# Causal attention with a soft mixture of experts: routing products moved to the idle score place, one maximum transposition for a pair of heads, a fourth buffer for raw q and k

## The chip, the cores and the metric

The kernel runs on one core of one Trainium2 chip. A core has five engines that run side by side and wait for each other by semaphores: TensorE (PE; its weight loads are listed apart as PEld), VectorE (DVE), ScalarE (ACT), GpSimd (POOL) and SyncE (SP), which here issues nearly all DMAs. SBUF holds the operands, and matrix products land in PSUM, which has eight banks of 512 float32 columns on 128 partitions. The metric is the device time of one execution in microseconds (us).

## The reference

```python
# q, k, v: (8, 12, 448, 64); phi: (768, 32); w1: (8, 768, 1024); w2: (8, 1024, 768)
scores = q @ k.T / 8, masked above the diagonal with -1e9       # each of 96 heads
attn = exp(scores - scores.max(-1)); attn /= attn.sum(-1) + 1e-9
x = (attn @ v), heads side by side                               # (3584, 768)
logits = x @ phi                                                 # (3584, 32)
d = softmax of logits over the 3584 rows;  slot_input = d.T @ x  # (32, 768)
slot_out = relu(slot_input @ w1[e]) @ w2[e]                      # 4 slots for each of 8 experts
out = (softmax of logits over the 32 slots) @ slot_out           # (3584, 768)
```

## The kernel before

Heads go in pairs: 48 pairs `p`, six for each of the eight batch rows, and one call of `block(p)` for each. Heads are numbered `i`; block `p` finishes heads `a = 2p` and `a + 1` and prepares heads `a + 2` and `a + 3`. `m6 = p % 6` says which of the six pairs of a batch row it is. Every engine runs its instructions in the order in which the code is written (`_InOrder`).

PSUM is full: three score places of two banks each (`s`, 1024 columns; head `i` uses place `i % 3`), one bank `po` for attention outputs, one bank `m` (`misc`) that all else shares in turn. A score place holds the keys on its partitions and the queries of a head on its columns (chunk 0 of the keys at columns 576 to 1023, chunks 1 to 3 at 0, 320 and 512).

For one block, in the order of the code:

- `scores2(a)`: four products that add the row maxima (negated, from `r2`) and a low part of q to the open scores of head `a` (in the profile `s<-r,k`). `exps(a)`: ScalarE's exponential of the place (`pt<-s`). `scores1_all(a + 2)`: causal mask (`s<-tri,identb`) and q-k products (`s<-qd,ks`) of head `a + 2` into the place that is free.
- `max_keys(a + 2, 0..2)` on VectorE: a transposing maximum over the place (`r<-s`), then two small ones (`r<-r`).
- The same for `a + 1` and `a + 3`. `xtrans(p - 1)` between them: the normalised output of the last pair is transposed into bank `m` (`xt`) and copied by ScalarE (`xts`).
- Preparing later pairs: `sub_q(p + 1)` and `sub_k(p + 2)` on GpSimd, the loads of raw q and k of pair `p + 3` (`load_qk`), `copy_k2`, `cast_q`, `cast_k` on ScalarE, in this order, ahead of the next block's exponential.
- `attv(a)`, `attv(a + 1)`, `attv3(p)`: attention outputs into `po`. Each listed product is two passes in the profile: 24, 24 and 16.
- The row maxima: `max_row(i, 0)` transposes the maxima of one head into bank `m` (`rt`), `max_row(i, 1)` takes the maximum over them (`mr<-rt`), `max_spread(i)` on GpSimd writes them into `r2` (`r<-mr`). In the kernel before, once for `a + 2` between `attv(a)` and `attv(a + 1)`, once for `a + 3` behind `attv3`.
- `norm(p, 0..2)` on VectorE: `sm` (denominators), a reciprocal, one wide product and two small ones (`x<-po,sm`).
- Routing, one part in most blocks: m6 = 2, 4, 0 form the logits (`g`, read by VectorE into `lt`); m6 = 1 exponentiates them (`logits_d`); m6 = 2 transposes both (`logits_e`: `tp`, copied by ScalarE to `gs` and `lg`); m6 = 3 and 5 form the experts' inputs (`sp`, added by VectorE into `si`). All of these products use bank `m`.

The raw q and k (`st["raw", ...]`) come from the pool `raw`, which gives its buffers out in turn; each pair takes one for k and one for q, k first. k is free after `sub_k`, q after `sub_q`. SyncE issues a block's loads in order: v of the next pair, in odd blocks a weight piece (`load_w`), k, q. After block 47 the experts run on weights that stream in.

Of the kernel before, what the change touches and what calls it, by code (L numbers as in the profile page):

```python
# [9 lines left out]
F32 = mybir.dt.float32  # L10
# [3 lines left out]
ALU = mybir.AluOpType  # L14
# [33 lines left out]
SC0, SC1, SC2, SC3 = 576, 0, 320, 512  # L48
RW, RC, RF = 96, 4, 20
NQ = 2 * NCH - 1  # L50
# [30 lines left out]
def attention_soft_moe(ctx: ExitStack, tc: tile.TileContext, qk, va, phi, w1, w2, out):  # L81
# [165 lines left out]
    def scores1(i, part):  # L247
        if i >= NHD:
            return
        p, h = divmod(i, 2)  # L250
        ks, qd = ks_[p % NR], qd_[p % NR]
        if ("s", i) not in st:
            st["s", i] = ps_s.tile([P, 1024], F32, tag="s", name=f"s{i}")
# [24 lines left out]
    def max_keys(i, k):  # L278
# [4 lines left out]
        if i >= NHD:  # L283
            return
        r = r_[i % 2]
        if k == 0:
            nc.vector.tensor_reduce(out=r[:, RC:RC + 72].rearrange("p (a b)->p a b", b=36)[:, :, 0:16],
                                    in_=st["s", i].rearrange("p (a b k)->p a b k", a=2, k=32),
                                    axis=AX.X, op=ALU.max, apply_transpose=True)
        elif k == 1:  # L290
            w = r[:, 0:84].rearrange("p (j q)->p q j", j=2)[:, 0:16]
            nc.vector.tensor_reduce(out=r[:, RF:RF + 76].rearrange("p (a q)->p a q", a=2)[:, :, 0:8],
                                    in_=w.rearrange("p (a q) j->p a q j", a=2), axis=AX.X, op=ALU.max)
        else:
            nc.vector.tensor_reduce(out=r[:, RF + 8:RF + NQB],
                                    in_=r[:, 14:80].rearrange("p (j q)->p q j", j=3)[:, 0:6],
                                    axis=AX.X, op=ALU.max)

    def max_row(i, k):
        if i >= NHD:  # L300
            return
        if k == 0:
            st["rt", i] = misc(f"rt{i}")
            nc.tensor.transpose(out=st["rt", i][0:AW, 0:P], in_=r_[i % 2][:, RF:RF + AW], identity=ident)
        else:
            mr = st["mr", i] = wk.tile([NQB, 32], F32, tag="mr", name=f"mr{i}", bufs=2)
            nc.vector.tensor_reduce(out=mr, in_=st.pop(("rt", i))[0:NQB, 0:P].rearrange("p (g t)->p t g", g=4),
                                    axis=AX.X, op=ALU.max, negate=True)

    def max_spread(i):  # L310
        if i >= NHD:
            return
        p, h = divmod(i, 2)
        mr = st.pop(("mr", i))

        nc.gpsimd.affine_select(out=r2_[p % NR][0:NQB, h].rearrange("p (b t)->p b t", t=32),
                                in_=mr.unsqueeze(1).to_broadcast([NQB, NQB, 32]),
                                compare_op=ALU.is_equal, fill=0.0, base=0,
# [104 lines left out]

    def logits_e(b):
        tp = misc(f"tp{b}")
        nc.tensor.transpose(out=tp[:, 0:P], in_=gs, identity=ident)
# [24 lines left out]

    def dispatch(b, hf):
        sp = misc(f"sp{b}_{hf}")
        dispatch_a(b, hf, sp)
        dispatch_b(b, hf, sp)

    warm(START[0], a=x_[1][:, NCH - 1, 0:AW].bitcast(BF16))
# [21 lines left out]
    for i, k in ((0, 0), (0, 1), (0, 2), (1, 0)):  # L479
        max_keys(i, k)  # L480
    sub_k(1, h0)
    max_row(0, 0)
    warm(START[5], pob[:, 0:2 * P])
    max_row(0, 1)
    max_spread(0)
    for k in (1, 2):
        max_keys(1, k)
    max_row(1, 0)
    max_row(1, 1)
    sub_k(1, h1, nc.vector)  # L490
    max_spread(1)
    cast_k(2)

# [26 lines left out]
    def block(p):  # L520
# [33 lines left out]
        if last:  # L554
            attv(a, [(qc, qc, FULL if qc < 3 else FULL[0:1]) for qc in range(NCH)], po0, begun)
            dispatch(NB - 2, 1)
            x, m = x_of(p), NCH - 1
# [355 lines left out]
```

## Time and profile before

| | |
|---|---|
| median of 3 runs | 449.91 us (448.70 to 450.89) |
| the profiled execution | 451.65 us, its span 449.9 us |
| busy, share of the span | PE 389.0 (86%), PEld 297.2 (66%), DVE 300.0 (67%), ACT 288.5 (64%), POOL 264.3 (59%) |
| mean granted TensorE clock | 0.981 |
| DMA | 119.16 MB, 265 GB/s on the mean |

Row times are microseconds from the span's start; a row of the timeline is start, duration, engine, line, operation, output from inputs, shapes, count, and in brackets the engine's idle time ahead of it with what ended it. All operations pass through one helper (line 65), so the names of the tiles tell them apart. In the text a block begins with its first `s<-r,k`; block 8 begins at 66.46 and block 47 at 343.49.

### The profile page before, as it was taken

The numbers are of one execution on the slowest core, as the hardware profiler recorded it, in microseconds if no ns is written. First come the engines' busy times: TensorE is split into PE (matmuls) and PEld (weight loads), VectorE is DVE, ScalarE is ACT, GpSimd is POOL, SyncE is SP. The second block draws the span as 40 slices with busy tenths as digits, with TensorE's granted clock in tenths as the row PEclk, the third lists the DMA queues.
The fourth block names the chain that finished last, engine by engine and source line by source line (L and its number), as shares of the span: only waits on it lengthen the run. The fifth ranks groups of instructions, "written<-read, shape, count | busy, mean of one in ns | idle before, by whom it ended". The sixth has DMA issues, their size and how long they took to land.

```text
span 449.9 us, 14022 instructions
## 1 busy us (share of the span) xinstructions
PE 389.0 (86%) x5763; PEld 297.2 (66%) x5763; DVE 300.0 (67%) x817; ACT 288.5 (64%) x400; POOL 264.3 (59%) x215
## 2 busy tenths in 40 slices
PE   6998799898999899989989999899999998977750
PEld 3786687777787678777777778777777554623330
DVE  6776677777687668767776778777876476422450
ACT  6788588777777767787678778877765111422340
POOL 5998778687787768778777787877872000000000
PEclk9999999999999999999999999999999999999985
DMA  7667776767776666676866678766684999999998
GB/s 266 220 211 236 230 230 215 218 219 237 253 218 205 231 214 224 203 228 217 262 211 201 224 234 259 235 202 218 219 263 148 391 419 422 427 423 410 403 396 351
DMA packets 34479, 119.16 MB, mean 265 GB/s; under 512 B 3824, under 2 KB 8944, under 8 KB 32880
## 3 DMA queue, kind: packets, MB, share of 16 engines
q1 hardware_dynamic: 34272, 118.01, 75.6%
q8 instruction: 45, 0.74, 0.7%
q10 hardware_dynamic: 144, 0.27, 0.2%
q14 instruction: 18, 0.15, 0.1%
HBM read 107.25 MB, written 11.01 MB: 263 GB/s over the span
## 4 chain that ended last, share of the span: by engine, by line
PE 48%; DMA 20%; DVE 9%; issue 7%; POOL 6%; ACT 6%; SPq 0%; DVEq 0%; POOLq 0%; ACTq 0%
PE s L65 17%; PE po L65 16%; DMA w<-in_w_dram 14%; DMA qk<-in_qk_dram 7%; POOL r L65 5%; DVE r L65 4%; PE xt L65 4%; PE rt L65 3%; ACT pt L65 3%; PE sp L65 2%; PE g L65 2%; DVE mr L65 2%; PE pp L65 1%; PE hp L65 1%; POOL ks L65 1%
## 5 line engine op out<-in xcount | busy, mean ns | idle before, releaser
L65 DVE TRANSPOSE_TENSOR_REDUCE r<-s 128x32 f32<-128x1024 f32 x96 | 119.9, 1249 | 32.3 <-PE s L65 31.4
L65 ACT ACTIVATE pt<-s 128x1024 f32<-128x1024 f32 x96 | 97.9, 1020 | 28.8 <-PE s L65 26.0
L65 PE MATMUL po<-va,pt 128*64 128x65 f32 x3040 | 111.1, 226 | 0.1
L65 PEld LDWEIGHTS po<-va,pt 128*64 128x64 f32 x3040 | 97.9, 139 | 17.9 <-issue 11.9
L65 POOL TENSOR_TENSOR r<-qk,qd 64x896 fp32r<-64x896 f32 (+1 forms) x49 | 101.3, 2068 | 7.3 <-ACT qd L65 3.6
L65 POOL TENSOR_SCALAR_AFFINE_SELECT r<-mr 14x448 fp32r<-14x448 f32 x96 | 61.8, 645 | 70.3 <-DVE mr L65 68.5
L65 POOL TENSOR_TENSOR ks<-qk,ks 64x896 fp32r<-64x896 f32 (+1 forms) x47 | 97.7, 2079 | 0.6 <-ACT ks L65 0.3
L65 PE MATMUL s<-qd,ks 128*66 128x64 f32 (+3 forms) x384 | 78.4, 315 | 2.6 <-DVE ks L65 1.9
L65 PEld LDWEIGHTS s<-r,k 128*128 128x128 f32 (+1 forms) x384 | 59.1, 175 | 20.4 <-POOL r L65 13.3
L65 PE MATMUL s<-r,k 128*128 128x448 f32 (+3 forms) x384 | 65.8, 294 | 3.6 <-POOL r L65 3.6
L65 ACT ACTIVATE ks<-qk 128x896 fp32r<-128x896 f32 (+1 forms) x50 | 45.6, 914 | 21.5 <-DMA qk<-in_qk_dram 19.2
L65 PEld LDWEIGHTS s<-qd,ks 128*128 128x128 f32 (+1 forms) x384 | 49.8, 181 | 4.0 <-DVE ks L65 2.4
L65 ACT ACTIVATE qd<-qk 128x896 fp32r<-128x896 f32 (+1 forms) x50 | 46.1, 922 | 1.7 <-DMA qk<-in_qk_dram 0.5
L65 ACT ACTIVATE xts<-xt 128x512 f32<-128x512 f32 x47 | 28.0, 597 | 29.2 <-PE xt L65 29.2
L65 ACT ACTIVATE k<-ks 64x896 fp32r<-64x896 f32 (+1 forms) x49 | 45.8, 934 | 1.2
L65 PE MATMUL s<-tri,identb 128*128 128x128 bf16 (+2 forms) x288 | 43.2, 235 | 3.2 <-ACT pt L65 3.2
L65 DVE TENSOR_REDUCE r<-r 128x16 f32<-128x32 f32 x192 | 33.7, 176 | 4.9
L65 PE MATMUL xt<-ident,x 128*128 128x128 f32 x188 | 29.9, 281 | 6.4 <-ACT lg L65 6.4
L65 PEld LDWEIGHTS <-identb 128*128 128x128 bf16 x320 | 27.2, 99 | 7.1 <-issue 5.3
L65 DVE TENSOR_TENSOR x<-po,sm 128x384 f32<-128x384 f32 (+2 forms) x49 | 26.7, 547 | 7.4 <-PE sp L65 6.0
L65 DVE TENSOR_REDUCE mr<-rt 14x32 f32<-14x128 f32 x96 | 25.7, 268 | 7.2 <-PE rt L65 1.0
L65 DVE TENSOR_SCALAR sm<-po 128x7 f32<-128x7 f32 (+1 forms) x48 | 7.9, 165 | 31.6 <-PE po L65 31.6
(137 smaller groups left out, 379.4 us busy)
## 6 DMA issues: line engine op xcount, KB each, us to landing
qk<-in_qk_dram SPq DMA_DIRECT2D x94, 448.0 KB, 3.7
w<-in_w_dram SPq DMA_DIRECT2D x43, 768.0 KB, 6.6
w<-in_w_dram SPq DMA_DIRECT2D x10, 1536.0 KB, 24.8
va<-in_va_dram SPq DMA_DIRECT2D x47, 260.0 KB, 3.9
out_dram<-ot SPq DMA_DIRECT2D x16, 384.0 KB, 6.7
out_dram<-ot SPq DMA_DIRECT2D x2, 1536.0 KB, 9.1
qk<-in_qk_dram SPq DMA_DIRECT2D x4, 224.0 KB, 3.4
hw<-in_w_dram SPq DMA_DIRECT2D x1, 768.0 KB, 12.2
```

What stands on the lines that cost most here:

```text
L65: return self._tc.keep_in_program_order(op(*args, **kwargs))
```

## The change

Four things, with the order of the instructions around them:

1. The three score places are allocated once (`s_`), and the routing products (`g`, `sp`, `tp`) go to place `(a + 1) % 3`, which is empty at a block's end, instead of bank `m`. That is the place that `scores1_all` of the next block fills first. `logits_e` moves from m6 = 2 (ahead of `xtrans`) to the end of m6 = 1.
2. The maxima of both heads of a pair lie in one tile `r`, 32 columns apart. `max_row` and its VectorE maximum are done once for the pair, on 46 rows, `rt` between `attv(a + 1)` and `attv3`; the two spreads follow each other on GpSimd.
3. `max_keys(a + 3, 1..2)` stands ahead of that transposition.
4. The pool `raw` has four buffers instead of three, so that k of pair `p + 3` takes the buffer of k of pair `p + 1`, and q that of q.

TensorE, block 11 (m6 = 5), from the end of the attention products to the next block's first mask product. Before (`s_1396` is the next block's first head, `s_1499` the place that is filled next):

```order
L65 MATMUL rt_1478<-ident,r_90 64x128 [waits DVE_49,PE_49]
L65 MATMUL sp_1_1483<-x_87,gs 32x384 [waits DVE_49]
L65 MATMUL sp_1_1483<-x_87,gs 32x384 x3
L65 MATMUL s_1396<-r_92,k_94 128x448 [waits Activation_49,Pool_49]
L65 MATMUL s_1396<-r_92,k_94 128x320
L65 MATMUL s_1396<-r_92,k_94 128x192
L65 MATMUL s_1396<-r_92,k_94 66x64
L65 LDWEIGHTS identb
L65 MATMUL s_1499<-tri,identb 128x128
```

The same stretch in the changed kernel (`s_87` is the place for both the routing products and the next scores):

```order
L65 MATMUL s_87<-x_90,gs 32x384 x4
L65 MATMUL s_85<-r_94,k_96 128x448 [waits Activation_49,Pool_49]
L65 MATMUL s_85<-r_94,k_96 128x320
L65 MATMUL s_85<-r_94,k_96 128x192
L65 MATMUL s_85<-r_94,k_96 66x64
L65 LDWEIGHTS identb
L65 MATMUL s_87<-tri,identb 128x128 [waits DVE_49]
```

The routing product has lost its wait for VectorE, and the first mask product has one now.

VectorE, the same block, from the second head's transposing maximum to the routing product's reader. Before:

```order
L65 TENSOR_REDUCE r_90<-s_1419 128x2x16 [waits PE_49]
L65 TENSOR_REDUCE mr_1463<-rt_1449 14x32 [waits PE_49,Pool_49]
L65 TENSOR_REDUCE r_90<-r_90 128x2x8 [waits DVE_49]
L65 TENSOR_REDUCE r_90<-r_90 128x6 [waits DVE_49]
L65 TENSOR_SCALAR sm_1476<-po 128x7 [waits PE_49]
L65 TENSOR_REDUCE mr_1480<-rt_1478 14x32 [waits PE_49,Pool_49]
L65 RECIPROCAL sm_1476<-sm_1476 128x7 [waits DVE_49]
L65 TENSOR_TENSOR x_101<-po,sm_1476 128x2x3x64 [waits DVE_49]
L65 TENSOR_SCALAR x_101<-po,sm_1476 64x64 x2
L65 SCALAR_TENSOR_TENSOR si<-si,al_1007,sp_1_1483 128x384 [waits PE_49]
```

The same stretch in the changed kernel:

```order
L65 TENSOR_REDUCE r<-s_86 128x2x16 [waits PE_49,Activation_49]
L65 TENSOR_REDUCE r<-r 128x2x8 [waits DVE_49]
L65 TENSOR_REDUCE r<-r 128x6 [waits DVE_49]
L65 TENSOR_REDUCE mr_1393<-rt_1383 46x32 [waits PE_49,Pool_49]
L65 TENSOR_SCALAR sm_1397<-po 128x7 [waits PE_49]
L65 RECIPROCAL sm_1397<-sm_1397 128x7 [waits DVE_49]
L65 TENSOR_TENSOR x_103<-po,sm_1397 128x2x3x64 [waits DVE_49]
L65 TENSOR_SCALAR x_103<-po,sm_1397 64x64 x2
L65 SCALAR_TENSOR_TENSOR si<-si,al_955,s_87 128x384 [waits PE_49,Activation_49]
```

One small maximum is left, ahead of the normalisation, and the reader of the routing product stays behind it.

ScalarE, blocks 7 and 8 (m6 = 1 and 2), from the k cast to the second exponential of block 8. Before:

```order
L65 ACTIVATE ks_86<-qk_10_1002 128x896 [waits PE_49,DMAHW5_49,Activation_49,Pool_49]
L65 ACTIVATE pt_96<-s_969 128x1024 [waits DVE_49,PE_49]
L65 ACTIVATE gs<-tp_1085 128x128 [waits PE_49]
L65 ACTIVATE lg<-tp_1085 128x128
L65 ACTIVATE run_z<-run_z,bs_1008,al_1007 128x1
L65 ACTIVATE xts_1096<-xt_1091 128x512 [waits PE_49]
L65 ACTIVATE pt_98<-s_992 128x1024 [waits DVE_49]
```

The same stretch in the changed kernel:

```order
L65 ACTIVATE ks_89<-qk_10_950 128x896 [waits PE_49,DMAHW5_49,Activation_49,Pool_49]
L65 ACTIVATE gs<-s_85 128x128 [waits PE_49]
L65 ACTIVATE lg<-s_85 128x128
L65 ACTIVATE run_z<-run_z,bs_956,al_955 128x1
L65 ACTIVATE pt_98<-s_86 128x1024 [waits DVE_49,PE_49]
L65 ACTIVATE xts_1038<-xt_1033 128x512 [waits PE_49]
L65 ACTIVATE pt_100<-s_87 128x1024 [waits DVE_49]
```

The copies of the transposed logits have moved ahead of the next block's first exponential.

The diff, cut to what the text speaks of:

```diff
-    raw = early.enter_context(tc.tile_pool(name="raw", bufs=3, side="right"))
+    raw = early.enter_context(tc.tile_pool(name="raw", bufs=4, side="right"))
...
-    ps_s = scs.enter_context(tc.tile_pool(name="ps_s", bufs=3, space=PSUM))
+    ps_s = scs.enter_context(tc.tile_pool(name="ps_s", bufs=1, space=PSUM))
+    s_ = [ps_s.tile([P, 1024], F32, name=f"s{i}") for i in range(3)]
...
-    r_ = [fix.tile([P, RW], F32, name=f"r{i}") for i in range(2)]
+    r_ = fix.tile([P, RW], F32, name="r")
...
-    def max_row(i, k):
-        if i >= NHD:
+    def max_row(p, k):
+        if p >= NPAIR:
             return
         if k == 0:
-            st["rt", i] = misc(f"rt{i}")
-            nc.tensor.transpose(out=st["rt", i][0:AW, 0:P], in_=r_[i % 2][:, RF:RF + AW], identity=ident)
+            st["rt", p] = misc(f"rt{p}")
+            nc.tensor.transpose(out=st["rt", p][0:AW, 0:P], in_=r_[:, 0:AW], identity=ident)
         else:
-            mr = st["mr", i] = wk.tile([NQB, 32], F32, tag="mr", name=f"mr{i}", bufs=2)
...
+            mr = st["mr", p] = wk.tile([AW, 32], F32, tag="mr", name=f"mr{p}", bufs=2)
+            nc.vector.tensor_reduce(out=mr[0:32 + NQB], axis=AX.X, op=ALU.max, negate=True,
+                                    in_=st.pop(("rt", p))[0:32 + NQB, 0:P].rearrange("p (g t)->p t g", g=4))
...
         scores2(a + 1, range(NCH))
-        if m6 == 2 and b >= 0 and p > 6:
-            logits_e(b)
         if p:
             xtrans(p - 1)
...
         attv(a, [(qc, qc, FULL) for qc in range(3)], po2, begun)
-        max_row(a + 2, 0)
         attv(a + 1, [(qc, 3 + qc, FULL) for qc in range(3)], po2, begun)
-        max_row(a + 2, 1)
-        max_spread(a + 2)
         for k in (1, 2):
             max_keys(a + 3, k)
+        max_row(p + 1, 0)
         attv3(p)
+        max_row(p + 1, 1)
+        max_spread(p + 1, 0)
+        max_spread(p + 1, 1)
         norm(p, 0)
-        max_row(a + 3, 0)
-        max_row(a + 3, 1)
-        max_spread(a + 3)
...
+        m = s_[(a + 1) % 3]
         if m6 in (3, 5) and p > 6:
-            sp = misc(f"sp{b}_{m6 // 5}")
-            dispatch_a(b, m6 // 5, sp)
+            dispatch_a(b, m6 // 5, m)
         for k in (1, 2):
             norm(p, k)
         if m6 in (3, 5) and p > 6:
-            dispatch_b(b, m6 // 5, sp)
-        if m6 in (2, 4) and p >= 2:
-            next_logits(p // 6, m6 - 2, misc(f"g{p}"))
+            dispatch_b(b, m6 // 5, m)
+        elif m6 == 1 and p > 6:
+            logits_e(b, m)
+        elif m6 in (2, 4):
+            next_logits(p // 6, m6 - 2, m)
         elif m6 == 0 and p:
-            next_logits(b, 4, misc(f"g{p}"))
+            next_logits(b, 4, m)
             logits_b(b, lt)
```

Ahead of block 0, too, the transposition now stands behind the maxima of both heads.

More of the change, by code (lines that the diff above doesn't have):

```diff
@@ L48 @@
 SC0, SC1, SC2, SC3 = 576, 0, 320, 512
-RW, RC, RF = 96, 4, 20
+RW, RC, RH = 244, 68, 52
 NQ = 2 * NCH - 1
@@ L252, in scores1 @@
         if ("s", i) not in st:
-            st["s", i] = ps_s.tile([P, 1024], F32, tag="s", name=f"s{i}")
+            st["s", i] = s_[i % 3]
             st["open"] = set()
@@ L284, in max_keys @@
             return
-        r = r_[i % 2]
+        r, f = r_[:, RC + RH * (i % 2) - 4:], r_[:, 32 * (i % 2):]
         if k == 0:
-            nc.vector.tensor_reduce(out=r[:, RC:RC + 72].rearrange("p (a b)->p a b", b=36)[:, :, 0:16],
+            nc.vector.tensor_reduce(out=r[:, 4:64].rearrange("p (a b)->p a b", a=2)[:, :, 0:16],
                                     in_=st["s", i].rearrange("p (a b k)->p a b k", a=2, k=32),
@@ L290, in max_keys @@
         elif k == 1:
-            w = r[:, 0:84].rearrange("p (j q)->p q j", j=2)[:, 0:16]
-            nc.vector.tensor_reduce(out=r[:, RF:RF + 76].rearrange("p (a q)->p a q", a=2)[:, :, 0:8],
+            n = RC + 18 + (RH - 32) * (i % 2)
+            w = r[:, 0:72].rearrange("p (j q)->p q j", j=2)[:, 0:16]
+            nc.vector.tensor_reduce(out=f[:, 0:2 * n].rearrange("p (a q)->p a q", a=2)[:, :, 0:8],
                                     in_=w.rearrange("p (a q) j->p a q j", a=2), axis=AX.X, op=ALU.max)
@@ L310, in max_spread @@
-    def max_spread(i):
-        if i >= NHD:
+            st["rt", p] = misc(f"rt{p}")
+            nc.tensor.transpose(out=st["rt", p][0:AW, 0:P], in_=r_[:, 0:AW], identity=ident)
+        else:
+            mr = st["mr", p] = wk.tile([AW, 32], F32, tag="mr", name=f"mr{p}", bufs=2)
+            nc.vector.tensor_reduce(out=mr[0:32 + NQB], axis=AX.X, op=ALU.max, negate=True,
+                                    in_=st.pop(("rt", p))[0:32 + NQB, 0:P].rearrange("p (g t)->p t g", g=4))
+    def max_spread(p, h):
+        if p >= NPAIR:
@@ L312, in max_spread @@
             return
[L313 to L317, printed above, removed]
+        mr, r = st["mr", p], slice(32 * h, 32 * h + NQB)
+        nc.gpsimd.affine_select(out=r2_[p % NR][r, h].rearrange("p (b t)->p b t", t=32),
+                                in_=mr[r].unsqueeze(1).to_broadcast([NQB, NQB, 32]),
                                 compare_op=ALU.is_equal, fill=0.0, base=0,
@@ L422, in logits_z, with logits_e @@
                                        in1=st.pop(("bs", b)), op0=ALU.mult, op1=ALU.add)
-    def logits_e(b):
-        tp = misc(f"tp{b}")
+    def logits_e(b, tp):
         nc.tensor.transpose(out=tp[:, 0:P], in_=gs, identity=ident)
@@ L450, in next_logits @@
         logits_t(j, m[:, 0:P])
[L452 to L455, printed above, removed]
     warm(START[0], a=x_[1][:, NCH - 1, 0:AW].bitcast(BF16))
@@ L481, in attention_soft_moe @@
     sub_k(1, h0)
+    for k in (1, 2):
+        max_keys(1, k)
     max_row(0, 0)
@@ L484, in attention_soft_moe @@
     max_row(0, 1)
[L485 to L489, printed above, removed]
+    max_spread(0, 0)
+    max_spread(0, 1)
     sub_k(1, h1, nc.vector)
-    max_spread(1)
     cast_k(2)
@@ L555, in block @@
             attv(a, [(qc, qc, FULL if qc < 3 else FULL[0:1]) for qc in range(NCH)], po0, begun)
-            dispatch(NB - 2, 1)
+            dispatch_a(NB - 2, 1, s_[(a + 2) % 3])
+            dispatch_b(NB - 2, 1, s_[(a + 2) % 3])
             x, m = x_of(p), NCH - 1
```

7 lines of the change are left out of this document (2 added, 5 removed).

## The prediction

> **What bounds the kernel now.** I read the split into stages first, then one batch of six blocks, then single blocks in order of time, then the waits.
>
> The windows view (us, busy time of each engine, granted TensorE clock, DMA share, GB/s) for blocks 0 to 7, 8 to 46 and all that follows, then for six undisturbed blocks, 31 to 36 (m6 = 1, 2, 3, 4, 5, 0), with their sum:
>
> ```profile
> 11.93:66.46 54.53, 47.93 (x780) 40.66 (x781) 39.76 (x106) 40.75 (x50) 46.18 (x44) 1.00 0.70 226
> 66.46:343.49 277.03, 253.80 (x4027) 208.93 (x4026) 207.59 (x556) 212.67 (x272) 211.08 (x156) 0.99 0.71 226
> 343.49:449.90 106.41, 78.80 (x920) 43.40 (x916) 45.10 (x138) 27.36 (x68) 0.28 (x2) 0.93 0.96 388
> ...
> 231.95:237.60 5.65, 5.65 (x96) 5.05 (x93) 4.70 (x14) 4.17 (x8) 4.90 (x4) 1.00 0.78 269
> 237.60:245.62 8.02, 6.96 (x111) 5.62 (x111) 5.89 (x18) 7.46 (x11) 5.99 (x5) 1.00 0.60 193
> 245.62:252.64 7.02, 6.58 (x104) 5.19 (x100) 4.69 (x14) 4.52 (x6) 5.59 (x6) 1.00 0.83 274
> 252.64:259.61 6.97, 6.52 (x112) 5.46 (x108) 5.87 (x16) 5.84 (x7) 5.31 (x4) 1.00 0.61 190
> 259.61:266.62 7.01, 6.57 (x104) 5.18 (x100) 5.39 (x16) 5.15 (x7) 5.59 (x6) 1.00 0.83 278
> 266.62:273.43 6.81, 6.37 (x113) 5.41 (x109) 5.31 (x15) 5.50 (x7) 5.34 (x4) 1.00 0.60 176
> sum 41.48, PE 38.64 PEld 31.90 DVE 31.85 ACT 32.62 POOL 32.72; mean PE 6.44 PEld 5.32 DVE 5.31 ACT 5.44 POOL 5.45
> ```
>
> TensorE is busy 38.64 of 41.48 us in these six, at full clock: no other engine passes 32.8. A batch of this kind takes 41.48. Blocks 8 to 46 hold seven each of m6 = 2, 3, 4 and six each of 5, 0, 1: 6 x 41.48 + 8.02 + 7.02 + 6.97 = 270.9, against 277.0 in the row. So 6.1 us are disturbances. They come from late q and k. In the table of waits and in block 20 (timeline):
>
> ```profile
> ACT ks L65 <- DMA qk<-in_qk_dram: 19.2, 20, 2.4
> SPq L65 <- POOL r L65: 135.0, 47, 6.4
> 152.28 0.95 ACT L65 ACTIVATE ks<-qk 128x896 fp32r<-128x896 f32 x1 [1.22 <-DMA qk<-in_qk_dram]
> ```
>
> ScalarE's k cast stands ahead of the next block's exponential, so a load that comes late enough holds up everything; the load is late because SyncE waits for a raw buffer until `sub_q` on GpSimd is through (135 us in 47 waits).
>
> The rest is one block's end. Block 36 (m6 = 0), timeline, from the first attention product to the next scores:
>
> ```profile
> 269.71 0.92 PE L65 MATMUL po<-va,pt 128*64 128x65 f32 x24
> 269.82 1.25 DVE L65 TRANSPOSE_TENSOR_REDUCE r<-s 128x32 f32<-128x1024 f32 x1
> 270.56 0.30 PE L65 MATMUL rt<-ident,r 128*64 128x128 f32 x1
> 270.79 1.39 PE L65 MATMUL po<-va,pt 128*64 128x65 f32 x40
> 271.18 0.38 DVE L65 TENSOR_REDUCE r<-r 128x16 f32<-128x32 f32 x2
> 272.11 0.30 PE L65 MATMUL rt<-ident,r 128*64 128x128 f32 x1
> 272.23 0.17 DVE L65 TENSOR_SCALAR sm<-po 128x7 f32<-128x7 f32 x1 [0.67 <-PE po L65]
> 272.52 0.28 DVE L65 TENSOR_REDUCE mr<-rt 14x32 f32<-14x128 f32 x1
> 272.73 0.18 DVE L65 RECIPROCAL sm<-sm 128x7 f32<-128x7 f32 x1
> 272.85 0.65 PE L65 MATMUL g<-xts,phi 128*32 128x128 f32 x16 [0.44 <-DVE mr L65]
> 272.87 0.64 POOL L65 TENSOR_SCALAR_AFFINE_SELECT r<-mr 14x448 fp32r<-14x448 f32 x1 [0.90 <-DVE mr L65]
> 272.94 0.56 DVE L65 TENSOR_TENSOR x<-po,sm 128x384 f32<-128x384 f32 x1
> 273.41 0.57 DVE L65 TENSOR_SCALAR x<-po,sm 64x64 f32<-64x64 f32 x2
> 273.43 0.73 PE L65 MATMUL s<-r,k 128*128 128x448 f32 x4
> 273.99 0.26 PE L65 MATMUL s<-tri,identb 128*128 128x128 bf16 x2
> 274.02 0.29 DVE L65 TENSOR_TENSOR lt<-g,lt 128x128 f32<-128x128 f32 x1
> 274.15 0.29 PE L65 MATMUL s<-tri,identb 128*128 128x256 bf16 x1
> ```
>
> Call 269.71 zero. The second `rt` stands at 2.40, and the routing product `g` waits 0.44 for `mr`, whose PSUM bank it takes. The next block's `s<-r` starts at 3.72 and its first mask product at 4.28. VectorE reads `g` only at 4.31 to 4.60 (`lt<-g`), behind the normalisation (`sm`, `x`); nobody waits for that, since the next user of the bank is `xt`, later.
>
> **The change, step by step**, in the same clock.
>
> *One `rt`, one `mr`.* TensorE loses one transposition, 270.79 - 270.56 = 0.23, and VectorE one `mr` of 0.28. But the single `rt` now needs both heads' maxima: the transposing maximum ends at 0.11 + 1.25 = 1.36, its two small reductions (0.38, and some 0.03 ahead) at 1.78, and `rt` starts at 1.83 (0.05 from VectorE to TensorE, as from `mr`'s end at 272.80 to `g`). TensorE alone would be there at 0.85 + 0.83 = 1.68. Of the 40 passes in 1.32 us, 16 belong to `attv3`: it runs from 2.06 (0.23 behind `rt`) to 2.59. `mr` starts 0.11 behind the end of `rt` (the 272.11 row lasts 0.30 and `mr` could have started at 272.52): 2.24 to 2.52. Its 46 rows instead of 14 I price at nothing, 0.27 to 0.29 by `mr` and by `lt` on 128 rows. GpSimd's spread follows 0.07 later, 2.59 to 3.23, and `s<-r` may start at 3.29. TensorE is free at 2.59 + 0.58 (`g`, 272.85 to 273.43) = 3.17: a new wait of 0.12, or 0.7 in a block without routing products, in place of the 0.44. The second head's spread ends at 3.9, before the mask and key products are through.
>
> *Routing products in the score place.* `g` no longer waits. But the first mask product writes that place, and in the new order it carries a wait for VectorE (or ScalarE). What VectorE has ahead of `lt`: `sm` 0.12 behind `attv3`, 2.71 to 2.88; the reciprocal 2.91 to 3.09; `x` 3.12 to 3.68; the two small products, which start 0.09 before `x` ends, 3.59 to 4.16; `lt` 4.20 to 4.49. The mask product comes at 4.54, where TensorE would have been ready at 3.29 + 0.57 = 3.86. This is the heart of the forecast: 0.68 us of waiting in such a block, and the mask product 0.26 later than the 4.28 of now.
>
> For the dispatch blocks and for the transposed logits, the rows of blocks 33 and 31 to 32:
>
> ```profile
> 246.20 0.26 PE L65 MATMUL s<-tri,identb 128*128 128x128 bf16 x2
> 248.72 0.92 PE L65 MATMUL po<-va,pt 128*64 128x65 f32 x24
> 251.86 0.85 PE L65 MATMUL sp<-x,gs 128*32 128x384 f32 x8 [0.45 <-DVE mr L65]
> 252.76 0.56 DVE L65 TENSOR_TENSOR x<-po,sm 128x384 f32<-128x384 f32 x1 [0.85 <-PE sp L65]
> 253.84 0.61 DVE L65 SCALAR_TENSOR_TENSOR si<-si,al,sp 128x384 f32<-128x384 f32 x1
> ...
> 235.04 0.92 PE L65 MATMUL po<-va,pt 128*64 128x65 f32 x24
> 238.34 0.94 ACT L65 ACTIVATE ks<-qk 128x896 fp32r<-128x896 f32 x1
> 239.18 1.00 ACT L65 ACTIVATE pt<-s 128x1024 f32<-128x1024 f32 x1
> 240.26 0.27 ACT L65 ACTIVATE lg<-tp 128x128 f32<-128x128 f32 x1
> 240.58 0.42 PEld L65 LDWEIGHTS xt<-ident,x 128*128 128x128 f32 x4 [0.77 <-ACT lg L65]
> ```
>
> From the first mask product to the next zero pass 248.72 - 246.20 = 2.52 us of TensorE, which the change leaves alone. With `si` (0.61) in the place of `lt`, m6 = 5 reaches the mask product at 4.86. In m6 = 3, `x` overwrites what `sp` reads and waits for its end (the 0.85 in the 252.76 row): `sp` 2.59 to 3.44, then 0.05, and everything behind moves to a mask product at 5.23. In m6 = 1 the logits' copies now stand behind the k cast, which starts 3.30 behind zero (238.34 - 235.04) and ends at 4.24; the second copy ends 0.35 behind the activation ahead of it (240.53 against 240.18) and TensorE goes on 0.05 later: 4.64. In m6 = 2 they are gone.
>
> So the block lengths become: `g` 4.54 + 2.52 = 7.06; m6 = 5 7.38; m6 = 3 7.75; m6 = 1 7.16; without routing 3.86 + 2.52 = 6.38. Six: 3 x 7.06 + 7.38 + 7.75 + 7.16 = 43.5, against 41.48.
>
> *Fourth raw buffer.* k of pair p+3 no longer waits for `sub_q` of the same block but for work of the block before, so it is asked for some 2 us earlier, behind v and, in odd blocks, a weight piece. I take all 6.1 us as gone. In an odd block v, a weight piece and k (128 x 520, 1536 and 896 floats) are 1.51 MB ahead of the cast; at the 274 GB/s and the 0.83 share of the 245.62 row, so 330 at full share, that takes 4.6 us, and the cast's turn in m6 = 1 comes 3.09 + 3.30 = 6.4 us into the block. Not all may be gained: 0 to 6.1.
>
> *Start.* The first `s<-r` waits for both heads, so one transposing maximum and its reductions more may stand ahead of it: between 0 and 1.25 + 0.38; I take 0.8, since half is overlapped.
>
> *Tail.* From 343.49 the same instructions run behind the same buffers, so it moves with the attention. The end streams weights (DMA share 0.96). One weight piece (0.79 MB) more or less in the buffers that come free early is worth 2.0 us at that row's 388 GB/s, either way; I take 0.
>
> *Sum.* Holds of blocks 7 to 45 set blocks 8 to 46: 19 x 7.06 + 7 x 7.75 + 6 x 7.38 + 7 x 7.16 = 282.8, against 277.0: +5.8. Blocks 0 to 7: 0.57 + 2.52 to the first zero, 4 x 6.38 + 3 x 7.06, and 3.29 at the end = 53.1, and 0.8 for the start, against 54.5: -0.6. Together +5.2 us on the profiled execution's 451.65, so 456.85; that one lies 1.74 above the median of the runs, and the forecast for the median is 449.9 + 5.2, rounded: 455.
>
> **Rivals.**
> *Loop free (faster).* If reading the place were done before 3.86, TensorE would run 3.29 + 0.57 + 2.52 = 6.38 in every block (6.46 with `sp`, whose 0.85 reaches a little past 3.29): 6.5 batches x 38.4 = 250 instead of 277, and some 3 less in the first eight: 420. It decides at 0.68 us: the reading would have to end that much earlier. For it speaks that TensorE is the busiest engine and is relieved of 0.23 + 0.44 a block; against it the VectorE rows above, none of which the change shortens.
> *Shorter hold (no change).* The first mask product writes columns 576 and up of the place, and the reading is of columns 0 to 383; the first product into that half is the one at 274.15, 0.16 behind 273.99. If only that one were held, or VectorE ran 0.16 ahead of my sum, 42 blocks (2, 4, 6, 7 and 8 to 45) would give back 6.7 us: 448.4. [...] Against it stands the order, where the wait is on the earlier product; the traces show no such place yet.
> *Loads still late.* If the share of the DMA engines, not the buffer, is what delays k (0.83 in odd blocks against 0.60 in even ones), the 6.1 us return: 461.
>
> **Numbers.** Forecast 0.60, with bounds of 451 to 460 (0 to 6.1 of the loads, 0 to 1.6 of the start, 2.0 of the tail, 0.1 us a block of the hold); shorter hold 0.17; loop free 0.08; loads late 0.15. The range reaches from just below the shorter hold to past the late loads: 447 to 463. Half a per cent, 2.2 us, is what a measurement here tells from no change (the runs lie from 448.7 to 450.9). Slower by more: 0.54 of the forecast's 0.60 and 0.14 of the late loads, 0.68. Within: 0.06, 0.10 of the shorter hold and 0.01, 0.17. Faster: the other 0.07 of the shorter hold and the 0.08, 0.15.
>
> **What would show it.** In the profile after: `rt` and `mr` 48 times; the mask product idle some 0.6 us a block behind VectorE's `lt` or `si`, and behind ScalarE's `lg` in m6 = 1; no `g` waiting for `mr`; the k cast's wait for the DMA down from 19.2 to a few us; blocks of 7.1, 7.4, 7.8 and 7.2 us. Blocks of 6.4 us, or mask products that wait for nothing, prove me wrong; so does a k cast that waits as before.

## Result: the changed kernel is 5.7% slower

The changed kernel takes 476.73 us (median of 4 runs, 473.54 to 477.83) against 450.40 us for the kernel before in the same session (448.70 to 453.37): a ratio of 1.057, with a 95% interval of 1.049 to 1.064. The profiled execution has a span of 475.8 us, 25.9 longer than the 449.9 of before.

The windows view of the changed kernel, with the columns and the stages of before (blocks 0 to 7, 8 to 46, all that follows), then the sum of six undisturbed blocks, 26 to 31 (209.67 to 254.20; m6 = 2, 3, 4, 5, 0, 1), which take 7.10, 7.45, 7.79, 7.46, 7.44 and 7.29:

```profile
14.33:76.03 61.70, 50.89 (x775) 43.43 (x775) 39.45 (x99) 41.52 (x50) 46.16 (x44) 0.94 0.56 188
76.03:369.00 292.97, 256.23 (x3985) 210.18 (x3985) 207.78 (x513) 211.23 (x271) 210.07 (x155) 0.99 0.62 209
369.00:475.80 106.80, 79.07 (x920) 43.42 (x916) 45.52 (x138) 27.43 (x68) 0.86 (x2) 0.93 0.97 393
...
sum 44.53, PE 39.16 PEld 32.08 DVE 32.04 ACT 32.77 POOL 32.64; mean PE 6.53 PEld 5.35 DVE 5.34 ACT 5.46 POOL 5.44
```

The start loses 2.4 us (14.33 against 11.93), blocks 0 to 7 lose 7.2 (61.70 against 54.53), blocks 8 to 46 lose 15.9 (292.97 against 277.03), the rest 0.4. Six undisturbed blocks take 44.53 instead of 41.48, with TensorE busy for 39.16 of them (38.64 before): of the 3.05 us added, 2.5 are idle time.

Whom TensorE waits for in blocks 8 to 46, and ScalarE's wait for late k over the whole span (table of waits: total us, times, longest):

```profile
PE s L65 <- DVE si L65: 12.5, 13, 1.1
PE s L65 <- DVE lt L65: 11.8, 19, 0.6
PE s L65 <- ACT lg L65: 4.8, 7, 1.9
...
ACT ks L65 <- DMA qk<-in_qk_dram: 6.3, 6, 1.6
```

The waits of `g` and `sp` for `mr` (14.7 us before) are gone, and 29.1 us of waiting for the readers of the score place have come. ScalarE's wait for k is down from 19.2 to 6.3.

Block 36 of the changed kernel (timeline), the stretch that was shown of before:

```profile
291.04 1.86 PE L65 MATMUL po<-va,pt 128*64 128x65 f32 x48
291.21 1.25 DVE L65 TRANSPOSE_TENSOR_REDUCE r<-s 128x32 f32<-128x1024 f32 x1
292.50 0.40 DVE L65 TENSOR_REDUCE r<-r 128x16 f32<-128x32 f32 x2
293.04 0.27 PE L65 MATMUL rt<-ident,r 128*64 128x128 f32 x1
293.24 0.69 PE L65 MATMUL po<-va,pt 128*64 128x65 f32 x16
293.42 0.28 DVE L65 TENSOR_REDUCE mr<-rt 46x32 f32<-46x128 f32 x1 [0.53 <-PE rt L65]
293.78 1.35 POOL L65 TENSOR_SCALAR_AFFINE_SELECT r<-mr 14x448 fp32r<-14x448 f32 x2 [2.02 <-DVE mr L65]
293.98 0.17 DVE L65 TENSOR_SCALAR sm<-po 128x7 f32<-128x7 f32 x1 [0.27 <-PE po L65]
294.41 0.56 DVE L65 TENSOR_TENSOR x<-po,sm 128x384 f32<-128x384 f32 x1
294.48 0.74 PE L65 MATMUL s<-r,k 128*128 128x448 f32 x4
295.49 0.29 DVE L65 TENSOR_TENSOR lt<-s,lt 128x128 f32<-128x128 f32 x1
295.83 0.25 PE L65 MATMUL s<-tri,identb 128*128 128x128 bf16 x2 [0.62 <-DVE lt L65]
```

With 291.04, the first attention product, as zero: `rt` 2.00, `mr` 2.38, the spreads 2.74, `s<-r` 3.44, `sm` 2.94, `x` 3.37, `lt` 4.45, and the first mask product at 4.79, after 0.62 us behind `lt`. The mechanism of this hold is the one that was forecast, each step 0.14 to 0.25 us later.

In blocks 4 to 6 something else happens. They take 27.8 us together (40.96 to 68.74; 24.4 before). Block 4's end, timeline:

```profile
47.20 0.78 POOL L65 TENSOR_SCALAR_AFFINE_SELECT sid<-sid 128x32 f32<-128x32 f32 x3 [0.22 <-POOL sid L65]
47.63 0.28 DVE L65 TENSOR_REDUCE mr<-rt 46x32 f32<-46x128 f32 x1 [0.53 <-PE rt L65]
48.07 2.08 POOL L65 TENSOR_TENSOR r<-qk,qd 64x896 fp32r<-64x896 f32 x1
50.22 1.35 POOL L65 TENSOR_SCALAR_AFFINE_SELECT r<-mr 14x448 fp32r<-14x448 f32 x2
50.91 0.74 PE L65 MATMUL s<-r,k 128*128 128x448 f32 x4 [2.20 <-POOL r L65]
```

`mr` is ready at 47.91, but GpSimd is not: behind the selects that build `sid` it does the next block's `sub_q` (48.07, 2.08 us) and only then the spreads. TensorE's `s<-r` waits 2.20 us. Block 5 has the same order: `sub_q` from 57.97, behind ScalarE's cast of q, the spreads from 60.12, and `s<-r` waits 2.33. In the kernel before, at the same place, only the second head's spread stood behind `sub_q`, and the first head's scores started without a wait:

```profile
43.98 0.64 POOL L65 TENSOR_SCALAR_AFFINE_SELECT r<-mr 14x448 fp32r<-14x448 f32 x1
44.70 2.10 POOL L65 TENSOR_TENSOR r<-qk,qd 64x896 fp32r<-64x896 f32 x1
45.15 0.73 PE L65 MATMUL s<-r,k 128*128 128x448 f32 x4
46.87 0.64 POOL L65 TENSOR_SCALAR_AFFINE_SELECT r<-mr 14x448 fp32r<-14x448 f32 x1
47.56 0.74 PE L65 MATMUL s<-r,k 128*128 128x448 f32 x4 [0.92 <-POOL r L65]
```

### The profile page after: what moved, and what is told of

The parts are those of the page before. It is cut to its first block, busy times and chain, and to the rows that moved or that the text cites. A ratio compares the mean times of both kernels' runs of the same rounds, so it can differ in the third digit from the quotient of the medians.

```text
span 475.8 us, 13852 instructions
## 1 busy us (share of the span) xinstructions
PE 395.8 (83%) x5715; PEld 301.8 (63%) x5715; DVE 301.4 (63%) x768; ACT 288.1 (61%) x400; POOL 264.5 (56%) x215
## 4 chain that ended last, share of the span: by engine, by line
PE 47%; DMA 16%; DVE 12%; issue 6%; ACT 4%; SPq 1%; POOL 0%; ACTq 0%; DVEq 0%
PE s L65 20%; PE po L65 17%; DMA w<-in_w_dram 13%; DVE x L65 6%; PE xt L65 4%; DMA qk<-in_qk_dram 3%; DVE sm L65 2%; PE rt L65 2%; DVE si L65 2%; PE pp L65 1%; DVE lt L65 1%; DVE r L65 1%; ACT k L65 1%; ACT gs L65 1%; PE hp L65 1%
## 5 line engine op out<-in xcount | busy, mean ns | idle before, releaser
L65 PE MATMUL po<-va,pt 128*64 128x65 f32 x3040 | 119.2, 226 | 0.8
L65 PEld LDWEIGHTS po<-va,pt 128*64 128x64 f32 x3040 | 100.2, 137 | 24.6 <-issue 11.9
L65 PE MATMUL s<-qd,ks 128*66 128x64 f32 (+3 forms) x384 | 80.7, 322 | 2.3 <-DVE ks L65 2.3
L65 PEld LDWEIGHTS s<-r,k 128*128 128x128 f32 (+1 forms) x384 | 60.6, 178 | 26.9 <-POOL r L65 24.4
L65 PE MATMUL s<-r,k 128*128 128x448 f32 (+3 forms) x384 | 67.0, 297 | 8.2 <-POOL r L65 8.2
L65 PEld LDWEIGHTS <-identb 128*128 128x128 bf16 x320 | 31.1, 100 | 38.1 <-issue 36.7
L65 PEld LDWEIGHTS s<-qd,ks 128*128 128x128 f32 (+1 forms) x384 | 51.6, 187 | 2.4 <-DVE ks L65 2.4
L65 PE MATMUL xt<-ident,x 128*128 128x128 f32 x188 | 31.1, 290 | 0.0
L65 DVE TENSOR_REDUCE mr<-rt 46x32 f32<-46x128 f32 x48 | 13.6, 282 | 25.5 <-PE rt L65 25.5
L65 DVE TENSOR_SCALAR x<-po,sm 64x64 f32<-64x64 f32 x94 | 26.2, 278 | 0.7
```

The source lines that it names most:

```text
L65: return self._tc.keep_in_program_order(op(*args, **kwargs))
```

## Experiments

The theory after this comparison: the loop lost through the hold of the first mask product, which VectorE's order sets; blocks 4 to 6 through GpSimd's order; the start through the wait for both heads. Rivals: that the pair itself made the loop slow, and that the early blocks and the start are accidents of one execution.

### The fourth buffer alone

On the kernel before:

```diff
-    raw = early.enter_context(tc.tile_pool(name="raw", bufs=3, side="right"))
+    raw = early.enter_context(tc.tile_pool(name="raw", bufs=4, side="right"))
```

> The kernel before with the fourth raw buffer alone. Theory: of the wait of the k cast for the DMA (19.2 us in the main loop) only some 6 us lie on TensorE's path, so the time falls by 3 to 8 us, to 442 to 447, and ScalarE's wait for k falls to a third or less, as it did with the whole change (19.2 to 6.3). Rival: the buffer is not what made the loads late, and the time stays at 450.

Measured 448.88 us against 452.67 of before beside it: 0.992 (0.989 to 0.994). Windows, blocks 8 to 46, and ScalarE's wait:

```profile
70.39:341.19 270.80, 251.81 (x4027) 207.67 (x4026) 207.45 (x556) 212.51 (x272) 211.06 (x156) 1.00 0.68 226
...
ACT ks L65 <- DMA qk<-in_qk_dram: 7.4, 10, 1.4
```

270.80 against 277.03: the 6.1 us of disturbances that the prediction had found are gone, to a tenth. Two expectations were missed: the time was to fall to 442 to 447, and ScalarE's wait for k to a third or less; it is 7.4 of 19.2. The median fell by 3.8 us only. In this profiled execution the first `s<-r` comes 2.9 us later (14.86, see the last experiment), and blocks 0 to 7 take 1.0 and all behind the loop 0.5 us more than in the first profile of before; how much of that the other executions share stays open.

### The pair alone

The kernel before with the shared tile `r`, one `rt`, one `mr` and two spreads in a row, routing products in bank `m`, three raw buffers:

```diff
 ...
         attv(a, [(qc, qc, FULL) for qc in range(3)], po2, begun)
-        max_row(a + 2, 0)
         attv(a + 1, [(qc, 3 + qc, FULL) for qc in range(3)], po2, begun)
-        max_row(a + 2, 1)
-        max_spread(a + 2)
         for k in (1, 2):
             max_keys(a + 3, k)
+        max_row(p + 1, 0)
         attv3(p)
-        norm(p, 0)
-        max_row(a + 3, 0)
-        max_row(a + 3, 1)
-        max_spread(a + 3)
+        max_row(p + 1, 1)
+        max_spread(p + 1, 0)
+        max_spread(p + 1, 1)
+        norm(p, 0)
```

> The kernel before with one transposition and one small maximum for both heads of a pair, nothing else. Theory: the main loop gets shorter, since the routing product and the scores wait for one maximum that is ready 0.4 us earlier than the second one was; by the rows of after a block with g is 3.43 + 0.57 + 2.49 = 6.5 long instead of 6.9 to 7.0, six blocks 40.2 instead of 41.48, so blocks 8 to 46 lose some 8 us. At the start 2.4 us are lost, and in blocks 4 to 6 some 5, since GpSimd's order has the q subtraction ahead of both spreads there: 447 to 453 in all. Rival (the pair itself is what made the loop slow, because everything waits for the later head): blocks 8 to 46 take 285 or more and the time is 460 or more.

Measured 451.93 us, 0.998 of before (0.995 to 1.002). Windows, six undisturbed blocks (24 to 29) and blocks 8 to 46:

```profile
184.86:225.24 40.38, 38.54 (x617) 31.73 (x613) 31.69 (x80) 32.95 (x42) 32.69 (x25) 1.00 0.73 234
74.57:341.99 267.42, 250.80 (x3987) 206.00 (x3988) 205.71 (x513) 212.25 (x271) 210.37 (x155) 1.00 0.74 232
```

Six blocks in 40.38 and the loop in 267.42: the pair by itself makes the loop 9.6 us shorter. In this execution it gives that back at the start (14.03, a point that lay at 11.93 and at 13.51 in two executions of the kernel before) and in blocks 0 to 7 (60.54; blocks 4 to 6 alone 28.4), where GpSimd's order is the same as in the changed kernel. That refutes the rival: the pair by itself does not make the loop slow.

### The score place alone

The kernel before with static places, `g`, `sp` and the transposed logits in place `(a + 1) % 3`, two `rt` and two `mr`, three raw buffers:

```diff
+        m = s_[(a + 1) % 3]
         if m6 in (3, 5) and p > 6:
-            sp = misc(f"sp{b}_{m6 // 5}")
-            dispatch_a(b, m6 // 5, sp)
+            dispatch_a(b, m6 // 5, m)
 ...
-        if m6 in (2, 4) and p >= 2:
-            next_logits(p // 6, m6 - 2, misc(f"g{p}"))
+        elif m6 == 1 and p > 6:
+            logits_e(b, m)
+        elif m6 in (2, 4):
+            next_logits(p // 6, m6 - 2, m)
```

> The kernel before with the routing products in the idle score place alone; two transpositions and two small maxima as before, three raw buffers. Theory: the first mask product is held until VectorE has read the place behind its normalisation, or ScalarE behind its k cast. With the second head's small maximum between, lt would end at 4.60 as in before, the mask product come at 4.65 instead of 4.28, and six blocks take 44.0 instead of 41.48: blocks 8 to 46 lose 13 to 17 us, and the time is 462 to 468. The start stays as before. Rival (the hold is hidden, the pair is the cause): 448 to 452.

Measured 464.55 us, 1.027 of before (1.021 to 1.033). Windows, six undisturbed blocks (36 to 41); TensorE's waits in blocks 8 to 46; and four rows of block 36:

```profile
276.16:319.92 43.76, 38.44 (x623) 32.22 (x619) 31.95 (x86) 32.87 (x43) 32.65 (x25) 1.00 0.71 218
...
PE s L65 <- DVE lt L65: 13.6, 19, 0.7
PE s L65 <- DVE si L65: 12.8, 13, 1.1
PE s L65 <- ACT lg L65: 9.5, 7, 2.1
...
280.22 0.92 PE L65 MATMUL po<-va,pt 128*64 128x65 f32 x24
282.73 0.17 DVE L65 TENSOR_SCALAR sm<-po 128x7 f32<-128x7 f32 x1 [0.62 <-PE po L65]
283.44 0.56 DVE L65 TENSOR_TENSOR x<-po,sm 128x384 f32<-128x384 f32 x1
284.86 0.24 PE L65 MATMUL s<-tri,identb 128*128 128x128 bf16 x2 [0.72 <-DVE lt L65]
```

Six blocks in 43.76 (44.0 expected, 41.48 before): the hold alone costs 2.3 us in six blocks. Blocks 8 to 46 take 287.6, 10.6 more than before where 13 to 17 were expected: their undisturbed blocks add 14.2, and late loads take 2.5 us instead of 6.1. The kernel's `sm` starts 2.51 behind the first attention product and its `x` 3.22, the mask product comes at 4.64; with the pair on top these are 2.94, 3.37 and 4.79, since `attv3` then stands behind the one `rt`, which waits for both heads' maxima. So the pair, which gains 1.1 us in six blocks with the products in bank `m` (41.48 to 40.38), loses 0.8 in the held place (43.76 to 44.53): there, the reading on VectorE sets the length, and the earlier `s<-r` is of no use.

### GpSimd's early order

The changed kernel with the five instructions that build `sid` moved ahead of the first spread, where GpSimd waits:

```diff
     sub_k(1, h0)
+    nc.gpsimd.memset(sid, 0.0)
+    for g in range(4):
+        nc.gpsimd.affine_select(out=sid, in_=sid, compare_op=ALU.not_equal, fill=1.0,
+                                base=-32 * g, pattern=[[-1, NSLOT]], channel_multiplier=1)
 ...
-             lambda: nc.gpsimd.memset(si, 0.0), lambda: nc.gpsimd.memset(sid, 0.0)]
-    later += [lambda g=g: sid_part(g) for g in range(4)]
+             lambda: nc.gpsimd.memset(si, 0.0)]
```

> The changed kernel with the five small GpSimd instructions that build sid moved from blocks 3 to 5 to the start, where GpSimd waits; GpSimd's order then has both spreads ahead of the next q subtraction in every block. Theory: blocks 4, 5 and 6 (9.95, 9.91 and 7.92 us) fall to 7.3, 6.5 and 7.3, the time by 5 to 7 us, to 470 to 472; the main loop stays at 293. Rival: the early blocks are long for another reason (the cold clock, or the loads), and the time stays within 2 us of 476.7.

Measured 468.95 us, 1.036 of before (1.033 to 1.039). Windows of blocks 0 to 7, and GpSimd at block 4's end:

```profile
14.45:68.68 54.23, 48.35 (x774) 41.07 (x774) 39.41 (x99) 41.60 (x50) 45.12 (x39) 1.00 0.65 214
...
46.89 1.35 POOL L65 TENSOR_SCALAR_AFFINE_SELECT r<-mr 14x448 fp32r<-14x448 f32 x2
48.67 2.10 POOL L65 TENSOR_TENSOR r<-qk,qd 64x896 fp32r<-64x896 f32 x1
```

The spreads now stand ahead of `sub_q`, blocks 0 to 7 take 54.23 instead of 61.70, and blocks 8 to 46 take 292.5 against 293.0. The time lies 1 us below what was expected, and blocks 4 to 6 take 6.52, 7.28 and 6.54. Five instructions of 1.1 us in all, none of them part of the change, had cost 7.5 us through the order in which they made the others stand. Of these, 2.5 are busy time of TensorE (50.89 against 48.35): behind each of the two long waits the changed kernel ran 3.4 us at half the clock (0.50), as the last section shows.

### Reading the place first

The kernel of the last experiment, with VectorE's `lt` and `si` ahead of the normalising products:

```diff
-        for k in (1, 2):
-            norm(p, k)
+        norm(p, 1)
         if m6 in (3, 5) and p > 6:
             dispatch_b(b, m6 // 5, m)
 ...
             next_logits(b, 4, m)
-            logits_b(b, lt)
+        norm(p, 2)
+        if m6 == 0 and p:
+            logits_b(b, lt)
```

> The changed kernel with the early sid instructions (469.0 us, blocks 8 to 46 in 292.5) and VectorE's reading of the score place (lt, si) moved ahead of the normalising products x, behind the reciprocal. Theory: TensorE's waits for lt and si (22.6 us in blocks 8 to 46) go almost wholly, the next bound is the single spread at s<-r, as in the pair alone (6.62 a block); only m6 = 1 keeps its wait for ScalarE. Blocks 8 to 46 come to 262 to 270 and the time to 439 to 447. Rival (the place is bad for another reason, the lost overlap of the maxima or the products themselves): x and with it xt come later by the time of lt, the wait moves there, and the time stays above 460.

Measured 446.36 us as the median of four runs, 445.18 without the slowest of them (448.27); without that one the ratio to before is 0.984 (0.975 to 0.992). That is 22.6 or 23.8 us less than the kernel it was made from (468.95, in another session). Windows of blocks 8 to 46, and TensorE's waits there:

```profile
67.56:336.35 268.79, 253.44 (x3986) 208.49 (x3986) 204.28 (x512) 211.24 (x271) 210.54 (x155) 0.99 0.68 227
...
PE s L65 <- ACT lg L65: 2.6, 3, 1.2
```

The waits for `lt` and `si` (24.3 us) are gone from the table, and with them 23.7 us of the loop (292.52 to 268.79). Nothing but the order of VectorE's instructions was changed: it is shown that the loss was the late reading on VectorE, and not the place as such. The wait for `lg` was to stay in every m6 = 1; it stayed in three, before blocks 8, 20 and 32, where the k cast ahead of the copies had waited for its load (by 0.73, 1.00 and 0.26 us).

### Routing products back in bank m

The same base (changed kernel, `sid` early), pair and four buffers kept:

```diff
-        m = s_[(a + 1) % 3]
+        m = misc(f"g{p}") if p > 1 and m6 != 1 and (m6 % 2 == 0 or p > 6) else None
 ...
+        if m6 == 2 and b >= 0 and p > 6:
+            logits_e(b)
         if p:
             xtrans(p - 1)
```

> The changed kernel with the early sid instructions and the routing products back in the shared PSUM bank, the transposed logits back in m6 = 2 ahead of xt; pair and four raw buffers stay. Theory: the gains of the parts add up once the place is out: six blocks 40.4 as with the pair alone (267.4 us for blocks 8 to 46, less the 4.4 us that still hung on late loads there), so 263 for blocks 8 to 46 and 437 to 441 in all. Rival (the parts do not add, the pair needs k earlier than the fourth buffer brings it): 445 to 450.

Measured 442.77 us, 0.979 of before (0.974 to 0.985). Blocks 8 to 46 take 266.9: 264.9 by its undisturbed blocks and 2.0 of late loads. I had taken 263 and no late loads; the median lies 1.8 us above my range, on the side of the sum of the parts rather than of the rival.

### The transposed logits early

As the last one, but the transposed logits at the end of m6 = 1 in the idle place, with ScalarE's copies ahead of the k cast:

```diff
 ...
-        cast_k(p + 3)
+        if m6 != 1 or p <= 6:
+            cast_k(p + 3)
 ...
+        elif m6 == 1 and p > 6:
+            logits_e(b, s_[(a + 1) % 3])
+            cast_k(p + 3)
```

> As the one with the routing products in the shared bank, but the transposed logits at the end of m6 = 1 in the idle place, with ScalarE's two copies ahead of the k cast instead of behind it. Theory: m6 = 2 loses the 0.8 us that tp and lg cost ahead of xt there, and m6 = 1 gains no wait, since the copies are done 0.8 us earlier than in after: 432 to 437. Rival: the k cast comes 0.7 us later, pushes the exponential behind it, and what is won in m6 = 2 is lost again: within 2 us of the kernel beside it.

Measured 437.40 us, 0.969 of before (0.963 to 0.975), just above the 432 to 437 that were expected. Windows, six undisturbed blocks (24 to 29) and blocks 8 to 46:

```profile
174.53:214.44 39.91, 38.46 (x617) 31.67 (x613) 31.75 (x80) 33.62 (x43) 32.76 (x25) 1.00 0.71 240
67.02:328.12 261.10, 250.18 (x3985) 205.80 (x3985) 205.88 (x513) 211.65 (x271) 210.70 (x155) 1.00 0.70 233
```

Blocks with m6 = 2 fall from 7.50 to 6.70 us and m6 = 1 stays at 6.63: 5.8 us less in the loop. Of the uses of the idle place tried here it is the one that beats the shared bank; its reader, ScalarE, is done early.

On the kernel that reads first the transposed logits stand at that place already; there, the k cast alone was moved behind the copies:

> As the one that reads first, but in m6 = 1 ScalarE's copies out of the place stand ahead of the k cast. Theory: the wait for lg (4.4 us) goes too: 4 to 5 us less than that one, 435 to 442. Rival: the k cast comes later and pushes the exponential, so no gain.

Measured 441.34 us, 0.977 of before (0.970 to 0.983): 5.0 less than without the edit (3.8 against the 445.18), and blocks 8 to 46 in 265.06, 3.7 less. Undisturbed m6 = 1 and 2 hardly change (6.85 and 6.77 to 6.86 and 6.71). The gain is in blocks 8, 20 and 32, which took 7.61, 9.31 and 7.14 us and now take 6.71 each: a k cast that waits for its load no longer holds the copies, and through them the place. At block 8 the cast started 0.34 us behind the block's first `s<-r` after waiting 0.73; now the copies are through by 0.37, and the cast starts at 0.53 without a wait. Block 20's gain holds more than the wait, since its 9.31 had a stretch at half the clock (0.50 from 151.30 to 154.71). Block 38, at 7.98, takes 1.2 of it back.

### The start

Two kernels of above once more, unchanged, in another execution:

> The kernel before, unchanged, profiled in another execution, to see what its start is worth. Theory: the first scores run now in 0.71 and now in 1.20 us whatever the kernel, so the first s<-r lies anywhere from 11.9 to 14.9, and blocks 8 to 46 repeat within 2 us of 277. Rival: the start is the kernel's own, and it lies at 11.9 again.

> The changed kernel, unchanged, profiled in another execution. Theory: block 32's 10.14 is a late load that can fall on another block, while the clean blocks repeat to 0.02 (7.29, 7.10, 7.45, 7.79, 7.46, 7.45) and blocks 4 to 6 are 27 to 28 us again. Rival: the long early blocks are an accident of one execution.

Measured 452.81 and 476.65 us. The kernel before has its first `s<-r` at 13.51 here (11.93 in the first profile) and blocks 8 to 46 in 276.3; the changed one at 13.00 (14.33) and 292.7, with blocks 4 to 6 in 28.3 us and its late loads on block 20 (9.37) instead of 32 (10.14). The clean blocks and the long early ones repeat; the start does not. The first scores of the two heads (timeline), the kernel before in this execution, then the changed one:

```profile
7.16 0.71 PE L65 MATMUL s<-qd,ks 128*128 128x192 f32 x3
9.23 1.20 PE L65 MATMUL s<-qd,ks 128*128 128x192 f32 x3
```

```profile
7.02 0.71 PE L65 MATMUL s<-qd,ks 128*128 128x192 f32 x3
8.42 0.71 PE L65 MATMUL s<-qd,ks 128*128 128x192 f32 x3
```

The last kernel is the fastest of above with pair 0 handled as before the change, one head after the other:

```diff
-    for k in (1, 2):
-        max_keys(1, k)
     max_row(0, 0)
     warm(START[5], pob[:, 0:2 * P])
     max_row(0, 1)
     max_spread(0, 0)
+    for k in (1, 2):
+        max_keys(1, k)
+    max_row(0, 0)
+    max_row(0, 1)
     max_spread(0, 1)
```

> The fastest so far (routing products in the shared bank, transposed logits early, 437.4) with the two heads of the very first pair handled one after the other, as before the change: two transpositions and two small maxima for pair 0 alone. Theory: with equally fast first products the pair costs 13.12 against 11.93 at the start, so this gives 1.2 us back: 435 to 437. Rival: the start is set by the clock of the first products, and the difference drowns: within 1 us.

Measured 435.88 us, 0.963 of before (0.956 to 0.971). It is the fastest kernel of all, but against the one without this edit the difference of 1.5 us is inconclusive: the two intervals overlap, and in the profiled executions the first scores took 0.71 and 1.20 here, 1.20 and 0.95 there.

## Why the prediction was wrong

The direction was right, and in the loop the mechanism and the place; the size was not, and in the first blocks the prediction missed a wait. The forecast was +5.2 us, the profile shows +25.9, and the difference of 20.7 comes from four terms (8.6, 6.8, 3.4 and 1.6) and 0.4 us behind the loop.

- *Blocks 0 to 7* were forecast at 1.4 us less than before and took 7.2 more. The step that failed is "4 x 6.38 + 3 x 7.06": it gave the early blocks the lengths of the main loop, without a look at what GpSimd does there besides. The description of the kernel that I worked from, that every engine follows the order of the code, does not hold for GpSimd's selects: in the order as compiled the `sid` selects and `sub_q` stand ahead of the spreads. Before the change only the second head's spread was behind `sub_q`, and it was needed later; with one `mr` for the pair both spreads are, and the first `s<-r` with them: it waited 2.20 and 2.33 us. With the `sid` instructions out of the way the stretch takes 54.2 us, 1.1 from the forecast.
- *The loop's clock.* Forecast 282.8 for blocks 8 to 46, 289.6 by the undisturbed blocks of the trace. The hold is at the place and behind the engines that were named, but the mask product comes at 4.79, not at 4.54. The transposing maximum starts 0.17 behind zero instead of 0.11, its small maxima end 0.44 behind it instead of 0.42, and `rt` starts 0.14 behind these instead of 0.05: 2.00 instead of 1.83. `attv3` follows 0.20 behind `rt` instead of 0.23, and `sm` 0.74 behind the start of `attv3` instead of 0.65: 2.94 instead of 2.71, and everything on VectorE follows. From one zero to the next this makes 0.21 to 0.23 us where VectorE reads the place, while behind ScalarE's copies the sum was 0.06 too long. Over all 39 blocks the mean error is 0.17 us a block, 6.8 in all, where the prediction had allowed 0.1 either way. Why each of these small gaps differs is not shown.
- *Late loads.* "I take all 6.1 us as gone" is exactly right for the fourth buffer alone (270.80). In the changed kernel 3.4 us remain in the first profile and 3.1 in the second, on blocks with m6 = 2. Part of the reason is the place again: the copies that free it stand behind the k cast in m6 = 1, so a late load holds TensorE in a second way, as blocks 8, 20 and 32 of the two kernels that read first show. Another part is TensorE's clock: of the 3.0 us that block 32 lost, 1.5 are a longer wait for `lg` (1.91 instead of 0.43), and behind it the granted clock was 0.50 from 256.81 to 260.21. What makes k late on just these blocks stays open.
- *Start.* Forecast 0.8, measured 2.4. With the first scores equally fast it is 13.00 against 11.93, so 1.1; the rest, 1.3, goes with TensorE's clock: in the first profile of before both heads' scores ran fast (0.71 each), in that of the changed kernel neither did (0.81 and 1.20); the granted clock from 6.50 to 10.50 us is 1.00 in the one and 0.64 in the other.

The rival of a shorter hold, by which only a later product would wait, is refuted by the row at 295.83: the first mask product carries the wait for `lt`, though it writes columns 576 and up and `lt` reads columns 0 to 127. The order of this kernel waits for the whole place. The loop-free rival needed VectorE to be done 0.68 us earlier. Reading first brings that for the logits (in block 36 of that kernel `lt` ends 3.89 behind zero, where it ended at 4.74), and blocks 8 to 46 came to 268.8, not 250. What stands behind the hold: `s<-r` starts at 3.44 instead of 3.29, behind `g` and the spread, so such a block takes 6.53 from zero to zero and not 6.38; `si` still ends at 4.42, and the mask product follows at 4.48 (6.98 behind m6 = 3 and 5); ScalarE's copies behind the k cast give 7.14; and 4.4 us are late loads, with a stretch at half the clock (0.50) in block 20.

The range failed because each bound was that of one term around its own estimate: the loop's 6.8 us passed its bound of 0.1 us a block, 3.9 in all, and the one term that had not been looked at, GpSimd's order in the first blocks, had no bound at all.

## What to carry to other kernels

An idle buffer is free only until its next writer comes: before a product is moved there, ask who reads it, and what that engine has ahead of the read; moving the read ahead of the normalisation was worth 23.7 us here without any change in the work. When two results are merged into one, everything that stood ahead of the later one now stands ahead of both, so look through each queue for the blocks that carry extra work, the first ones above all. Parts of a change do not add: in blocks 8 to 46 the pair gained 9.6 us, the buffer 6.2, the place lost 10.6, and together they lost 15.9; with the place out for all but the early transposed logits, and one GpSimd order mended, the same parts give 0.969 of the time before.

## What was not expected of the hardware

TensorE's first scores (three products of 128x192) took 0.71 or 1.20 us in different executions of one and the same kernel, and the first `s<-r` of the kernel before came at 11.93 in one and 13.51 in the other. That alone is about a third of the spread of its runs (448.70 to 453.37). The first clock record of the trace, one of full clock, begins at 5.88 us in the first of these executions and at 4.44 in the second; what sets that point is not shown. In the second execution of the kernel before, the second head's products (1.20 us, from 9.23) lie in a stretch at half the clock (0.50, third number from the end):

```profile
7.86:11.27 3.41, 3.41 (x14) 1.84 (x12) 2.41 (x4) 2.77 (x6) 2.27 (x2) 0.50 0.86 307
```

That column can mislead. In the kernel with the fourth buffer alone both heads' products took 1.20 us, while the windows view gives 1.00 for that stretch:

```profile
6.50:10.50 4.00, 3.39 (x14) 2.25 (x15) 2.17 (x4) 3.45 (x7) 2.27 (x2) 1.00 1.00 384
```

The first clock record of that trace lies at 13.37 us, and the view counts time without a record as full clock, as it does ahead of 5.88 us in the first profile of before. A start is therefore compared by the durations of its products, or over several executions.

The clock also fell later, behind long waits. In the changed kernel, after the waits of 2.20 and 2.33 us in front of blocks 5 and 6:

```profile
52.01:55.41 3.40, 3.40 (x18) 3.10 (x16) 1.61 (x3) 1.69 (x3) 1.74 (x1) 0.50 0.75 295
62.25:65.65 3.40, 3.40 (x22) 2.85 (x22) 1.78 (x4) 1.95 (x4) 1.40 (x1) 0.50 0.47 185
```

In the first of these stretches the transposition `xt` took 1.10 us, where it has 0.63 in block 31. So more was lost at these two waits than their own length. Not at every wait: the kernel before waited 1.87 us in block 6 and stayed at 1.00. What decides it is open.
